# A decayed linear-attention and gated-MLP kernel: split evictions of a PSUM tile, second-product parts in any order, and a new order of all steps

## Chip, cores and metric

The kernel runs on one core of one Trainium2 chip. The metric is the time of one execution in device microseconds. A core has five engines with a queue each, worked through in order: TensorE (PE in the profile, its weight loads PEld), VectorE (DVE), ScalarE (ACT), GpSimd (POOL) and SyncE (SP), which here only issues transfers. POOL issues transfers too; the profile counts both kinds against the same 16 DMA engines.

## The reference, cut to what matters

```python
def _attn_ref(q, k, v, alpha):            # each (4, 8, 768, 48)
    for t in range(S):
        state = alpha[:, :, t, :, None] * state + einsum('bhd,bhe->bhde', k[:, :, t], v[:, :, t])
        y[:, :, t] = einsum('bhd,bhde->bhe', q[:, :, t], state)

def _moe_ref(x, w_in, w_out):             # x (3072, 384), w_in (384, 2048), w_out (2048, 384)
    h = x @ w_in
    g = h * np.cos(h)
    return g @ w_out
```

The output y of the recurrence, heads side by side, is the x of the two products.

## The kernel before

The 3072 rows are worked through as 12 pairs J of 256 rows, three pairs to a batch. A pair consists of two chunks c of 128 rows. Steps of a pair, with the engine that does them:

- `load` (SP): the four inputs a (alpha), k, q, v, 384 KB each. Tiles of a have 4 buffers, those of k, q and v 3 each, so a later load waits until a buffer has been read.
- `w1`, `w2` (POOL): each weight matrix in four loads, cast to bf16 on the way. The number in the plan is the quarter, not the pair.
- `mula` (POOL), `ln` (ACT), `cums0`/`cums` (PE), `sub` (DVE), `icp`, `exps` or together `eb` (ACT): the decay as running sums of logarithms, and its exponentials. `eb` also does the next pair's `ln`.
- `sk`, `sq` (POOL or DVE): k and q scaled by them; `castv` (POOL): v to bf16; `vst` (SP, by transfers inside the core) or `vpe` and `vev` (PE and ACT): v in another layout.
- `trans` (PE) transposes scaled q and k of both chunks into one PSUM tile T_ps of two banks, a bank for each chunk; `evT 0` and `evT 1` copy the banks into qkT, on ACT or DVE.
- `scores` (PE), `mask` (DVE): products of a chunk with itself; `outer` (PE), `add` (DVE), `decay`, `state` (POOL): the state that goes from chunk to chunk.
- `yT` (PE) sums what comes from state and scores into a tile y_ps of two banks; `evy 0` and `evy 1` copy the banks into xT.
- `m1 u` (PE, L361): a quarter u of the first product, 12 matmuls into a PSUM tile h_ps of two banks; `sin` (ACT, L367) takes its cosine as a shifted sine, `gate` (DVE, L372) multiplies the two into gsb.
- `m2 c part` (PE, L390): a quarter of the second product of chunk c, 4 matmuls that add up in o_ps; `evo` copies o_ps to o_sb (ACT or DVE), `out` stores it (SP). The last chunk has two half-width tiles o_last, and is stored in two halves.

The two-bank tiles (T_ps, y_ps, h_ps, U_ps, scores, the early sums) share three PSUM buffers, o_ps has one buffer, and later sums and half of o_last have one. A step that needs a buffer waits for whoever read it last. Two instructions of different engines that use one tile are kept in order by the tile framework.

The order is written out by hand in `PLAN`: each row is a step, each column a pair, and all steps are issued in the order of these numbers (a suffix :A, :D picks ACT or DVE; "-" means that the pair has no such step). A number has no meaning on the chip beyond that order: each engine takes its own steps in turn and waits for data and buffers. `idle` issues matmuls of zeros that keep the TensorE clock up while it has nothing else to do. ACT holds one set of function tables at a time: a `sin` behind an exponential or logarithm, and the other way round, costs a table load (`act_set`).

`GATES` ties the load of a[2] to the last matmul of yT[1]. SP's queue is in order, so every load behind it waits as well:

```python
    GATES, AFTER = {("a", 2): ("yT", 1)}, {}
```

The functions are those of this code:

Of the kernel before, what the change touches and what calls it, by code (L numbers as in the profile page):

```python
# [9 lines left out]
FP = mybir.dt.float32  # L10
# [6 lines left out]
def kernel(  # L17
# [81 lines left out]
    GATES, AFTER = {("a", 2): ("yT", 1)}, {}  # L99
    src = {"a": alpha, "k": k, "q": q, "v": v}  # L100

# [149 lines left out]
    T_ps, A_ps, y_ps, U_ps = {}, {}, {}, {}  # L251

    def trans(J):
        T_ps[J] = ps.tile([C, 2, 2 * NP, 2, HC], BF, tag="h", name="T_ps", bufs=3)
        for i, x in ((1, kh_t[J % NQ]), (0, qh_t[J % NQ])):
            for p in range(NP):
                for e in range(2):
                    for c in range(2):
                        r = slice(HC * c, HC * c + HC)
                        nc.tensor.transpose(T_ps[J][:, c, i * NP + p, e, :],  # L260
                                            x[r, e, 2 * p : 2 * p + 2, :].rearrange("s h d -> s (h d)"), ident_bf[r, r])

    def evict_T(J, c, copy):
        if J not in qkT_sb:
            qkT_sb[J] = sb.tile([C, 2, 2 * NP, C], BF, tag="qkT", name="qkT", bufs=BUF["qkT"])
        copy(out=qkT_sb[J][:, c], in_=T_ps[J][:, c].rearrange("r n e s -> r n (e s)"))  # L266

    def scores(J, c):
        qkT = qkT_sb[J]
        A_ps[J, c] = ps.tile([C, 2, NP, C], FP, tag="h", name="A_ps", bufs=3)  # L270
        for p in range(NP):
            for a in range(2):
                r = slice(64 * a, 64 * a + D)
                nc.tensor.matmul(A_ps[J, c][:, a, p, :], qkT[r, c, NP + p, :], qkT[r, c, p, :], start=True, stop=True)  # L274
# [42 lines left out]
    def yT(J):  # L317
# [25 lines left out]
        for key, step in GATES.items():  # L343
            if step == ("yT", J):
                AFTER[key] = last

    def evict_y(J, c, copy):
        if J not in xT:
            xT[J] = sb.tile([C, KT, T2], BF, tag="xT", name="xT", bufs=BUF["xT"])

        copy(out=xT[J][:, :, c * C : (c + 1) * C].rearrange("r i (t e) -> r i e t", e=2),  # L351
             in_=y_ps[J][:, c, 0 : KT * C].rearrange("r (i e t) -> r i e t", i=KT, e=2))

# [22 lines left out]

    def mlp2(J, c, part):
        if (J, c) == (NJ - 1, 1):
            if part == 0:

                o_ps[J, c] = [ps.tile([C, 512], FP, tag="x", name="o_last", bufs=1), two_banks("o_last")[:, 0]]
            for z, cols in enumerate(HALVES):
                for ft in range(part * NF // MP, (part + 1) * NF // MP):
                    nc.tensor.matmul(o_ps[J, c][z][:, 0 : DM // 2], gsb[J][:, ft, c * C : (c + 1) * C], w2[:, ft, cols],  # L384
                                     start=(ft == 0), stop=(ft == NF - 1))
            return
        if part == 0:
            o_ps[J, c] = ps.tile([C, 512], FP, tag="o", name="o_ps", bufs=1)
        for ft in range(part * NF // MP, (part + 1) * NF // MP):
            nc.tensor.matmul(o_ps[J, c][:, 0:DM], gsb[J][:, ft, c * C : (c + 1) * C], w2[:, ft],  # L390
                             start=(ft == 0), stop=(ft == NF - 1))

    def evict_o(J, c, copy):
# [6 lines left out]
        else:  # L400
            t = sb.tile([C, DM], FP, tag="o_sb", name="o_sb", bufs=4)
            copy(out=t, in_=o_ps.pop((J, c))[:, 0:DM])  # L402
# [9 lines left out]
    def idle(n):  # L412
# [132 lines left out]
```

## Time and profile before

| | us |
|---|---|
| median of 3 runs | 188.44 (188.35 to 189.09) |
| span of the profiled execution | 186.5 |
| TensorE busy in that span | 176.7 |
| ACT and DVE busy | 126.5 and 135.4 |

The span runs from the first to the last instruction of the profiled execution; the runs are timed around it and are some 2 us longer. How time is shared between the two products and the rest, from the page's costliest groups (busy us, mean ns of one, then the idle time of the engine just before them and what ended it):

```profile
L361 PE MATMUL h_ps<-xT,w 128*128 128x256 bf16 x576 | 66.7, 273 | 1.3 <-ACT xT L351 0.7
L390 PE MATMUL o_ps<-w,gsb 128*128 128x384 bf16 x368 | 66.7, 327 | 0.1
L266 ACT COPY qkT<-T_ps 128x1024 bf16<-128x1024 bf16 x8 | 8.0, 1015 | 6.9 <-PE T_ps L260 4.4
L266 DVE COPY qkT<-T_ps 128x1024 bf16<-128x1024 bf16 x16 | 10.8, 678 | 1.1 <-ACT qkT L266 1.1
L351 ACT CAST xT<-y_ps 128x384 bf16<-128x384 f32 x12 | 6.7, 594 | 5.6 <-PE y_ps L340 3.8
L351 DVE CAST xT<-y_ps 128x384 bf16<-128x384 f32 x12 | 6.8, 584 | 4.7 <-PE y_ps L340 2.9
```

A matmul's own time (273 ns) is its way through the array; matmuls overlap, so 12 of them in a row take 1.31 us, and a busy TensorE need not be one at its peak. Where TensorE waits a little, the gap is better read from the starts of its matmuls than from its idle time. The shape of the span, in 40 slices of 4.66 us, each digit a tenth:

```profile
PE   7988799989989999999999999999999999999993
PEclk9999999999999999999999999999999999999999
DMA  6999999999949979996799932600041005301102
```

### The profile page before, as it was taken

How to read it: one execution, taken by the hardware profiler on the slowest of the kernel's cores; microseconds unless marked ns; L12 is line 12 of the kernel's file. 1: busy time of each engine (PE TensorE's matmuls, PEld its weight loads, DVE VectorE, ACT ScalarE, POOL GpSimd, SP SyncE). 2: the span in 40 equal slices, each digit the busy share in tenths (PEclk: the TensorE clock that was granted, in tenths of full speed). 3: DMA queues.
4: the chain of work that ended last, by engine and by line, in shares of the span. 5: the costliest groups of instructions: out<-in, count | busy, mean ns of one | idle time of the engine just before them, and what ended most of it. 6: DMA issues, size and time to landing. Idle time of an engine off the chain costs nothing.

```text
span 186.5 us, 5746 instructions
## 1 busy us (share of the span) xinstructions
PE 176.7 (95%) x2467; PEld 126.4 (68%) x2469; DVE 135.4 (73%) x184; ACT 126.5 (68%) x161; POOL 77.1 (41%) x110
## 2 busy tenths in 40 slices
PE   7988799989989999999999999999999999999993
PEld 2434588655667786785688668676867686786872
DVE  7178775589799979698847987794977556754461
ACT  2466876889498986889668999728965264373330
POOL 5079510257645653781896076930360320100000
PEclk9999999999999999999999999999999999999999
DMA  6999999999949979996799932600041005301102
GB/s 152 261 258 165 181 204 237 259 266 265 274 105 304 264 180 245 264 260 167 186 278 278 247 104 46 182 0 4 4 136 47 5 0 158 118 0 66 64 0 84
DMA packets 60137, 29.47 MB, mean 158 GB/s; under 512 B 51024, under 2 KB 60112, under 8 KB 60112
## 3 DMA queue, kind: packets, MB, share of 16 engines
q1 hardware_dynamic: 56256, 25.86, 57.2%
q0 software_dynamic: 3712, 3.15, 11.0%
q8 instruction: 19, 0.31, 0.7%
q10 hardware_dynamic: 144, 0.10, 0.2%
q14 instruction: 6, 0.05, 0.1%
HBM read 25.17 MB, written 4.72 MB: 160 GB/s over the span
## 4 chain that ended last, share of the span: by engine, by line
PE 73%; ACT 15%; DVE 8%; issue 3%; DVEq 0%
PE h_ps L361 31%; PE o_ps L390 24%; PE idle_ps L416 4%; PE y_ps L340 3%; ACT qkT L266 3%; DVE gsb L372 3%; PE T_ps L260 2%; ACT c_sb L367 2%; PE A_ps L274 2%; ACT L136 2%; ACT cp L200 2%; PE U_ps L291 2%; DVE kh L212 2%; ACT icp L192 2%; PE o_last L384 1%
## 5 line engine op out<-in xcount | busy, mean ns | idle before, releaser
L372 DVE TENSOR_TENSOR gsb<-h_ps,c_sb 128x1024 bf16<-128x1024 f32 x48 | 58.1, 1221 | 21.9 <-ACT c_sb L367 21.2
L367 ACT ACTIVATE c_sb<-h_ps,halfpi 128x1024 bf16<-128x1024 f32 x48 | 53.0, 1113 | 26.8 <-PE h_ps L361 23.0
L361 PE MATMUL h_ps<-xT,w 128*128 128x256 bf16 x576 | 66.7, 273 | 1.3 <-ACT xT L351 0.7
L390 PE MATMUL o_ps<-w,gsb 128*128 128x384 bf16 x368 | 66.7, 327 | 0.1
L361 PEld LDWEIGHTS <-w 128*128 128x128 bf16 x576 | 55.6, 98 | 10.1 <-issue 1.6
L390 PEld LDWEIGHTS <-gsb 128*128 128x128 bf16 x368 | 33.8, 98 | 21.2 <-DVE gsb L372 0.6
L313 POOL TENSOR_TENSOR un<-us,c 128x384 bf16<-128x384 f32 x20 | 16.7, 835 | 40.7 <-DVE us L305 29.1
L279 DVE TENSOR_TENSOR A_sb<-A_ps,msk 128x1024 bf16<-128x1024 f32 x24 | 28.9, 1215 | 1.7 <-PE A_ps L274 1.7
L212 POOL TENSOR_TENSOR kh<-k,icp 128x384 bf16<-128x384 f32 x17 | 16.9, 999 | 9.2 <-ACT icp L192 7.8
L216 POOL TENSOR_TENSOR qh<-q,cp 128x384 bf16<-128x384 f32 x15 | 15.0, 1006 | 11.8 <-ACT cp L200 11.8
L149 POOL TENSOR_TENSOR a<-a 128x384 f32<-128x384 f32 x9 | 9.0, 1001 | 12.6 <-DMA a<-in_alpha_dram 12.6
L219 POOL CAST vp<-v 128x768 bf16<-128x768 f32 x12 | 10.1, 841 | 8.8 <-DMA v<-in_v_dram 7.7
L416 PE MATMUL idle_ps<-zeros 128*128 128x512 bf16 x38 | 12.0, 457 | 1.4 <-DVE zeros L52 1.2
L141 ACT ACTIVATE lna<-a 128x768 bf16<-128x768 f32 x12 | 10.2, 847 | 4.6 <-DMA a<-in_alpha_dram 4.6
L266 ACT COPY qkT<-T_ps 128x1024 bf16<-128x1024 bf16 x8 | 8.0, 1015 | 6.9 <-PE T_ps L260 4.4
L136 ACT ACT_TABLE_LOAD x9 | 11.5, 1283 | 0.9 <-PEq L529 0.7
L367 ACT ACT_TABLE_LOAD x9 | 11.5, 1283 | 0.2
L266 DVE COPY qkT<-T_ps 128x1024 bf16<-128x1024 bf16 x16 | 10.8, 678 | 1.1 <-ACT qkT L266 1.1
L305 DVE TENSOR_TENSOR us<-U_ps,un 128x384 f32<-128x384 f32 x16 | 8.7, 550 | 3.8 <-PE U_ps L291 2.8
L402 DVE COPY o_sb<-o_ps 128x384 f32<-128x384 f32 x12 | 6.6, 551 | 6.5 <-PE o_ps L390 6.5
L351 ACT CAST xT<-y_ps 128x384 bf16<-128x384 f32 x12 | 6.7, 594 | 5.6 <-PE y_ps L340 3.8
L351 DVE CAST xT<-y_ps 128x384 bf16<-128x384 f32 x12 | 6.8, 584 | 4.7 <-PE y_ps L340 2.9
(69 smaller groups left out, 159.1 us busy)
## 6 DMA issues: line engine op xcount, KB each, us to landing
k<-in_k_dram SPq DMA_DIRECT2D x12, 384.0 KB, 6.0
a<-in_alpha_dram SPq DMA_DIRECT2D x12, 384.0 KB, 6.1
v<-in_v_dram SPq DMA_DIRECT2D x12, 384.0 KB, 6.0
q<-in_q_dram SPq DMA_DIRECT2D x12, 384.0 KB, 6.3
out_dram<-o_sb SPq DMA_DIRECT2D x23, 192.0 KB, 2.6
vs<-vp SPq DMA_DIRECT2D x36, 64.0 KB, 2.1
w<-in_moe_w_out_dram POOLq DMA_DIRECT2D x4, 384.0 KB, 10.1
w<-in_moe_w_in_dram POOLq DMA_DIRECT2D x4, 384.0 KB, 7.3
```

The lines of the kernel that those rows point to most:

```text
L136: nc.scalar.preload_act_table_set("natural_log_exp_and_others")
L212: eng.tensor_tensor(out=kh_t[J % NQ][:, e, :, 0:D], in0=kqv["k", J][:, :, e], in1=icp_, op=ALU.mult)
L216: eng.tensor_tensor(out=qh_t[J % NQ][:, e, :, 0:D], in0=kqv["q", J][:, :, e], in1=cp, op=ALU.mult)
L266: copy(out=qkT_sb[J][:, c], in_=T_ps[J][:, c].rearrange("r n e s -> r n (e s)"))
L279: nc.vector.tensor_tensor(out=A_sb[J][:, c].rearrange("s a p t -> s (a p) t"), in0=A_ps.pop((J, c)).rearrange("s a p t -> s (a p) t"), in1 ...
L313: nc.gpsimd.tensor_tensor(out=u, in0=U_sum.pop(n), in1=c2_sb[J][:, :, c].unsqueeze(3).to_broadcast([C, NP, 2, D]), op=ALU.mult)
L351: copy(out=xT[J][:, :, c * C : (c + 1) * C].rearrange("r i (t e) -> r i e t", e=2), in_=y_ps[J][:, c, 0 : KT * C].rearrange("r (i e t) -> ...
L361: nc.tensor.matmul(h_ps[J, u][:, f, :], w1[:, kk, ft * C : (ft + 1) * C], xT[J][:, kk, :], start=(kk == 0), stop=(kk == KT - 1))
L367: nc.scalar.activation(out=c_sb[J, u], in_=h_ps[J, u], func=AF.Sin, bias=halfpi, scale=1.0)
L372: nc.vector.tensor_tensor(out=gsb[J][:, u * FW : (u + 1) * FW], in0=h_ps.pop((J, u)), in1=c_sb.pop((J, u)), op=ALU.mult)
L390: nc.tensor.matmul(o_ps[J, c][:, 0:DM], gsb[J][:, ft, c * C : (c + 1) * C], w2[:, ft], start=(ft == 0), stop=(ft == NF - 1))
L416: nc.tensor.matmul(idle_ps[0], zeros[:, 0:C], zeros, start=True, stop=True)
```

## The change

Four things, in the diff below.

1. `apart` tells the tile framework that the copies of a tile's two banks do not depend on each other where two engines do them (evict_T and evict_y).
2. `mlp2` counts the parts of a chunk that have been issued: the first to come starts the sum and takes the tile, the fourth ends it. Before, part 0 had to be first and part 3 last. (The tile of o_ps is now kept in a list; `evict_o` takes the first.)
3. `GATES` is empty: no load waits for a step of TensorE. Its use is moved to `pass_gate`, which may also be tied to a scores step; with no gate it does nothing.
4. Every row of `PLAN` has new numbers, and the engine of some evictions and scalings is another. `evT` is on ACT 10 times (8 before), `evy` 9 times (12 before), `evo` 13 times (11 before); `sk` and `sq` are on POOL 36 times (32 before). The two evictions of a pair are on two engines in 13 of 24 cases. There are 33 idle matmuls (38 before), and 14 changes of ACT's tables (18 before).

```diff
-    GATES, AFTER = {("a", 2): ("yT", 1)}, {}
+    GATES, AFTER = {}, {}
+    def pass_gate(step, last):
+        for key, gate in GATES.items():
+            if gate == step:
+                AFTER[key] = last
...
+    evicts = {}
+    def apart(key, copy, ins):
+        if key in evicts and evicts[key][0] != copy:
+            tc.declare_no_dep(ins.ins, evicts[key][1].ins, reason="two engines each evict a bank of their own")
+        evicts[key] = copy, ins
...
     def evict_T(J, c, copy):
-        copy(out=qkT_sb[J][:, c], in_=T_ps[J][:, c].rearrange("r n e s -> r n (e s)"))
+        ins = copy(out=qkT_sb[J][:, c], in_=T_ps[J][:, c].rearrange("r n e s -> r n (e s)"))
+        apart(("T", J), copy, ins)
...
     def evict_y(J, c, copy):
-        copy(out=xT[J][:, :, c * C : (c + 1) * C].rearrange("r i (t e) -> r i e t", e=2),
+        ins = copy(out=xT[J][:, :, c * C : (c + 1) * C].rearrange("r i (t e) -> r i e t", e=2),
              in_=y_ps[J][:, c, 0 : KT * C].rearrange("r (i e t) -> r i e t", i=KT, e=2))
+        apart(("y", J), copy, ins)
...
     def mlp2(J, c, part):
+        last_tile = (J, c) == (NJ - 1, 1)
+        done = parts_done[J, c] = parts_done.get((J, c), 0) + 1
+        if done == 1:
+            if last_tile:
                 o_ps[J, c] = [ps.tile([C, 512], FP, tag="x", name="o_last", bufs=1), two_banks("o_last")[:, 0]]
+            else:
+                o_ps[J, c] = [ps.tile([C, 512], FP, tag="o", name="o_ps", bufs=1)]
+        fts = range(part * NF // MP, (part + 1) * NF // MP)
+        for o, cols in zip(o_ps[J, c], HALVES if last_tile else [slice(0, DM)]):
+            for ft in fts:
+                nc.tensor.matmul(o[:, 0 : cols.stop - cols.start], gsb[J][:, ft, c * C : (c + 1) * C], w2[:, ft, cols],
+                                 start=(done == 1 and ft == fts[0]), stop=(done == MP and ft == fts[-1]))
...
 PLAN = {
-    "load a": "1320 1974 27415 27985 34270 40270 43270 54870 67336 68770 70970 93397",
-    "load k": "750 2544 28555 37270 46270 52480 58570 69470 72470 85140 91627 113474",
-    "load q": "5250 6750 29125 38770 48970 56370 57870 60070 78470 84570 87104 96187",
-    "load v": "3750 8250 35770 41770 51910 61570 67906 73970 75470 85710 95267 96757",
-    "w1": "15334 12769 17804 16954",
-    "w2": "11919 20284 19434 21134",
-    "evT 0": "14773:A 18473:A 41585 48048 60976 71899 81566:A 93894 111044 116949:A 129834 138061",
-    "evT 1": "16453:A 19403:A 43330 48048:A 59896 72979 81586 93289 112124 117657 128759 137201:A",
-    "yT": "20503 26545 48000 58219 72693 91349 90719 109104 124433 140168 151138 162701",
-    "evy 0": "21333:D 27535:D 49128:D 60501:D 73683 92814:D 91919 110094:D 125423 140998 152879:D 163777:D",
-    "evy 1": "21333 27658 48990 59421:D 73683:D 92339:D 91549 110569:D 125793 141368 152128 163814",
-    "m1 0": "23356 30719 52864 63871 77482 95445 98081 113200 130658 146436 158652 170128",
-    "m1 1": "22038 32037 51246 65489 74546 94127 92809 121714 129340 147754 154722 171446",
-    "m1 2": "27430 29401 54182 61235 78800 96763 104369 120396 132629 149072 159970 166198",
-    "m1 3": "25132 33355 55500 62553 76164 99399 110564 111882 136796 145118 161288 172764",
-    "m2 0 0": "28748 41460 56818 70639 84360 100717 114518 125318 138114 150390 163586 174082",
-    "m2 0 1": "34673 42113 57471 71292 85013 101670 115171 125971 138767 152023 164239 176046",
-    "m2 0 2": "35326 42766 59519 71945 85666 103063 116824 128034 139420 153416 164892 176699",
-    "m2 0 3": "35979 44554 60172 73893 86619 103716 117477 128687 140893 154069 165545 177352",
-    "evo 0": "36832:D 45407 61581:D 78353:D 87472 105178:D 118330 129540 141746 154922:D 166398:D 178205:D",
-    "out 0": "47770 53670 76970 97327 92197 114044 134921 150722 154222 155552 167028 178835",
-    "out 1": "44770 66136 87674 100827 112274 133721 136121 156752 149522 168228 170958 180161",
...
+    "load a": "30 10 560 580 900 1370 1560 2530 2620 3110 3750 2320",
+    "load k": "180 340 620 940 1570 2140 2680 2440 3280 4470 4150 4200",
+    "load q": "250 390 780 1050 1390 2370 2120 2930 3580 2270 3480 4870",
+    "load v": "70 530 890 1360 1530 3210 3020 3140 3850 4400 4660 4420",
+    "w1": "440 300 660 520 - - - - - - - -",
+    "w2": "1100 930 980 760 - - - - - - - -",
+    "evT 0": "290:A 490:A 1460:A 1720 2260 2800 3100:A 3620 4330 4620:A 5060:A 5520",
+    "evT 1": "360 480:A 1400 1700:A 2250 2750 3170 3600:A 4350 4640 5090 5530:A",
+    "yT": "510 740 1730 2110 2770 3640 3630 4300 5020 5210 5670 5950",
+    "evy 0": "590:D 810:D 1790:D 2130:D 2790 3690 3660:D 4320:D 5040 5240 5680 5980:D",
+    "evy 1": "540 750:D 1740:D 2210:D 2820:D 3700 3670:D 4310:D 5030:D 5250:D 5730 6020",
+    "m1 0": "790 860 1960 2490 2980 3790 3920 4550 5170 5620 5870 6380",
+    "m1 1": "720 1060 1800 2510 2850 3710 3680 4920 5370 5840 6160 6080",
+    "m1 2": "850 1030 2000 2230 3030 3860 4170 4910 5390 5920 5890 6270",
+    "m1 3": "840 970 2040 2410 2950 3940 4490 4440 5180 5600 6050 6260",
+    "m2 0 0": "1110 1420 2070 2710 3310 3990 4690 5340 5700 6100 6330 6520",
+    "m2 0 1": "1090 1540 2050 2840 3320 3960 4530 5080 5590 6120 6310 6500",
+    "m2 0 2": "1070 1500 2180 2740 3330 4020 4710 5350 5820 6130 6340 6490",
+    "m2 0 3": "990 1380 2280 2730 3270 4130 4720 5120 5720 6070 6350 6550",
+    "evo 0": "1130:D 1550 2300:D 2910:D 3410 4160 4730:D 5360 5830:D 6140:D 6360 6570",
+    "out 0": "3260 2390 2760 4480 3720 4830 6320 5970 6410 6290 6370 6580",
+    "out 1": "3390 2290 3070 4970 4000 5000 5460 5490 6150 6250 6510 6610",
...
 }
-IDLE = [(1501, 16), (7915, 1), (9416, 8), (12569, 4), (14554, 5), (16389, 3), (18254, 3)]
+IDLE = [(45, 14), (215, 9), (415, 6), (465, 1), (505, 1), (695, 2)]
```

In the new order SP's queue begins a1, a0, v0, k0, q0, k1, q1, v1, a2, a3, k2, q2, v2, a4, k3, q3, v3, a5 (before: k0, a0, a1, k1, v0, q0, q1, v1, then the gate, a2, a3, k2, q2, a4). The weights come as w1 quarters 1, 0, 3, 2 and w2 quarters 3, 1, 2, 0 (before: w2[0], then w1 1, 0, 3, 2, then w2 2, 1, 3). TensorE's first units and parts after yT[0] are m1.1[0], yT[1], m1.0[0], m1.3[0], m1.2[0], m1.0[1], m1.3[1], m2.0.3[0], m1.2[1], m1.1[1], m2.0.2[0], m2.0.1[0], m2.0.0[0], cums0[2].

More of the change, by code (lines that the diff above doesn't have):

```diff
@@ L273, in scores @@
                 r = slice(64 * a, 64 * a + D)
-                nc.tensor.matmul(A_ps[J, c][:, a, p, :], qkT[r, c, NP + p, :], qkT[r, c, p, :], start=True, stop=True)
+                last = nc.tensor.matmul(A_ps[J, c][:, a, p, :], qkT[r, c, NP + p, :], qkT[r, c, p, :], start=True, stop=True)
+        pass_gate(("scores", J, c), last)
     def mask(J, c):
@@ L342, in yT @@
             begun.add((c, g))
-        for key, step in GATES.items():
-            if step == ("yT", J):
-                AFTER[key] = last
+        pass_gate(("yT", J), last)
     def evict_y(J, c, copy):
@@ L375 @@
     HALVES = [slice(0, DM // 2), slice(DM // 2, DM)]
+    parts_done = {}
     def mlp2(J, c, part):
-        if (J, c) == (NJ - 1, 1):
-            if part == 0:
+        last_tile = (J, c) == (NJ - 1, 1)
+        done = parts_done[J, c] = parts_done.get((J, c), 0) + 1
+        if done == 1:
+            if last_tile:
                 o_ps[J, c] = [ps.tile([C, 512], FP, tag="x", name="o_last", bufs=1), two_banks("o_last")[:, 0]]
[L382 to L391, printed above, removed]
+            else:
[5 more added lines that the diff above has]
+                                 start=(done == 1 and ft == fts[0]), stop=(done == MP and ft == fts[-1]))
     def evict_o(J, c, copy):
@@ L401, in evict_o @@
             t = sb.tile([C, DM], FP, tag="o_sb", name="o_sb", bufs=4)
[L402 removed]
+            copy(out=t, in_=o_ps.pop((J, c))[0][:, 0:DM])
             o_sb[J, c] = [(t, slice(0, DM), nc.sync)]
```

2 lines of the change are left out of this document (1 added, 1 removed), and 84 rows, old and new, of the table PLAN.

## The prediction, made before the changed kernel ran

> **What bounds the kernel now.** I read the page's busy table first, then the busy time by stage, then the chain of waits, then what the transfers did in the first 40 us.
>
> ```profile
> PE 176.7 (95%) x2467; PEld 126.4 (68%) x2469; DVE 135.4 (73%) x184; ACT 126.5 (68%) x161; POOL 77.1 (41%) x110
> ...
> 0.00:22.20 22.20, 18.24 (x242) 9.18 (x245) 14.46 (x41) 12.03 (x19) 13.15 (x31) 1.00 1.08 205
> 22.20:36.85 14.65, 14.36 (x168) 11.72 (x168) 9.17 (x10) 11.77 (x11) 1.82 (x2) 1.00 1.25 229
> 36.85:53.34 16.49, 15.06 (x252) 9.55 (x252) 14.76 (x20) 13.01 (x22) 8.56 (x12) 1.00 1.05 250
> 53.34:120.00 66.66, 65.68 (x974) 49.04 (x973) 54.88 (x70) 56.90 (x71) 42.51 (x52) 1.00 0.89 213
> 120.00:186.50 66.50, 63.33 (x833) 46.92 (x832) 42.09 (x47) 32.78 (x40) 11.05 (x15) 1.00 0.15 48
> ```
>
> The columns after the stretch are PE, PEld, DVE, ACT, POOL, clock, DMA share and GB/s. TensorE sets the end. The clock is full throughout, and from 53 us on TensorE idles about 1 us before the last matmul. The change removes no real matmul (only 38 to 33 idle ones, all before 22 us), so all it can move is when the first h_ps matmul starts (22.20), what the transfers hold up before 53 us, and the small stalls behind. DMA share 1.25 and 1.05 says that the 16 engines are saturated between 22 and 53 us: whatever is loaded earlier makes something else later.
>
> The waits of one evicting engine for the other, and two of the stalls that end at TensorE:
>
> ```profile
> ACT qkT L266 <- DVE qkT L266: 2.4, 1, 2.4
> ACT xT L351 <- DVE xT L351: 1.8, 3, 0.8
> DVE xT L351 <- ACT xT L351: 1.8, 2, 1.1
> DVE qkT L266 <- ACT qkT L266: 1.1, 2, 0.9
> PE h_ps L361 <- ACT xT L351: 0.7, 1, 0.7
> PE U_ps L291 <- DVE xT L351: 0.6, 1, 0.6
> ```
>
> **Eviction pairs.** These rows add up to 7.1 us of one engine waiting for the other, but only 0.7 + 0.6 us arrive at TensorE by name: at 22.20 (DVE evicts xT from 20.94 for 0.59, ACT only from 21.56 for 0.59, then h_ps) and at 52.07. In the new order 13 of the 24 qkT and xT pairs are split over two engines. No row shows two engines reading one tile's two banks at once. Bounds: a pair ends with the slower copy (1015 ns on ACT beside 678 on DVE; 594 beside 584 for xT), or, if they hinder each other fully, as late as now, a gain of nothing. I take the first; each copy has a bank of its own.
>
> **The start.** Each input load takes 1.5 us (393 KB at 261 GB/s, the rate between 9 and 13 us). By place in the queue they land in before at 4.42, 5.94, 7.45, 8.95, 10.44, 11.95, 13.46. In the new order a1, a0, v0, k0, q0, k1, q1, v1: k0 waits until 8.95 instead of 4.42, q0 comes at 10.44 instead of 11.95. Walk with the durations of before: ln[0] ends 6.80 as now; icp.0, exps.0 of pair 0 and exps.0 of pair 1 run before the second-bank sums, and the sums wait for them (tile dependence, in the built program's waits), so exps.1[0] ends about 9.6 and icp.1[0] 11.1. DVE then does sk.1, sq.1, sq.0 of pair 0 (0.55 each) to 12.75; trans[0] ends 13.2 (now 14.32), scores.0[0] waits for ACT's evT.0 (1.02) and vev (0.8), both at 15.05 (now 16.11); the masks (1.21 each) end 18.2; yT[0] ends 19.0 (now 20.91). mask.0[1], which frees the bank, ends at 20.8, so the first h_ps matmul is possible at 20.85: 1.35 us earlier. This is the gain that the idle matmuls, the split evictions and the load order give together.
>
> **The gate that goes.** GATES held the load of a[2], and with it every later load on SP's queue, until yT[1]. Without it SP issues a2, a3, k2, q2, v2, a4 ... without a pause, and the eight weight loads on POOL's queue meet them. Before had them apart:
>
> ```profile
> 27.24 0.99 SPq L105 DMA_DIRECT2D a<-in_alpha_dram  x2
> ...
> 18.89 2.29 POOL L127 DMA_DIRECT2D w<-in_moe_w_out_dram  x3
> ...
> q0 software_dynamic: 624, 0.47, 131.4%
> ...
> q1 hardware_dynamic: 614, 0.23, 107.9%
> q0 software_dynamic: 9, 0.01, 5.5%
> ```
>
> The first two lines are the issues (SP's input loads, POOL's last weight loads); the third is the queue table between 28.4 and 30.7 us, weights alone; the last two between 31.6 and 32.4. A weight load is 512 packets of 768 B, so alone it takes 512 / (624 / 2.3) = 1.89 us; one engine sends a packet each 59 ns (2300 x 16 / 624). In the last window one engine still has weights, and beside the input packets it sends 9 in 800 ns, one each 89 ns: the queues alternate there packet by packet. Then a weight load takes 512 / 16 x 89 = 2.85, say 2.9 us with inputs beside it, and meanwhile the inputs get 512 packets of 384 B, half a load.
>
> The Trainium skill ("DMA: Bandwidth & Descriptors", Queues, rings and completion order) says each DMA engine goes round robin between queues at packet granularity. The last window agrees (89 ns); the earlier window does not: loads issued at 27.24 had no packet by 30.7. By the rule alone the weights would take the 2.9 us worked out above.
>
> POOL's new order is castv[0] (from 7.5), decay, sk.0[0] (to 10.9), then w1[1]; its packets start about 2 us after the issue (12.45 to 14.1 in before). The next two weights stand behind state.0[0], decay[1], sk.1[1], sq.0[1] (add.0[0] ends 13.25; then 0.85 + 0.25 + 1.0 + 1.0 give 16.4), the fourth behind castv[1] and state.1[0], the others behind the next states. So w1[1] comes at 16.5, in time; the other seven flow from about 19 us, 7 x 2.9 = 20.3, to 39.3, with 0.4 to land: w1[0] 22.3, w1[3] 25.2, w1[2] 28.1, w2[3] 31.0, w2[1] 33.9, w2[2] 36.8, w2[0] 39.7. In before the last lands at 32.8 (issued at 20.42, 12.4 us). TensorE does m1.1[0], yT[1], m1.0[0] to 24.7, waits for w1[3] and w1[2], runs five units and one part to 35.25, waits for w2[2] and for w2[0]; m2.0.0[0] (0.65) ends at 40.35, and only then cums0[2] follows, in before at 36.85. **Term 1: +3.5 us**, with the 1.35 of the start swallowed by it. Queued behind the waiting matmuls is all of TensorE; ACT and DVE starve with it.
>
> **36.85 to 53.34.** Here before pays for the gate: gaps between matmul starts are 3.0 us (0.8 before trans[2]'s q half, 0.75 before U_ps at 52.07, the rest 0.1 to 0.3 each). In the new one a2, a3, k2, q2, v2 have landed by then; the total of bytes is the same, so k3 and q3 come where they came (42.7 and 44.2; k3 at 42.99 in before, q3 about 1.5 later). Walked from 40.35 in the new order, TensorE waits for sq.0[2] behind exps.0[2] (0.3), for sq.0[3] behind mask.1[2] on DVE (0.5) and for evT.0[3] (0.2): 1.0 instead of 3.0. **Term 2: -2.0.**
>
> **The rest.** From 53 us the gaps between starts come to 2.1 us in before (0.43 at 76.5 for the second xT eviction, 0.52 at 86.4 and 0.46 at 119.6 for a late gate behind qkT evictions and table loads, the rest under 0.3). The split pairs and 14 instead of 18 switches between exponent and sine tables (4 x 1283 ns of ACT, hidden in the last stretch, where ACT is busy 32.78 of 66.5) take those away: -2.1. New ones: the order is dense and much is moved at once, q[9] is loaded before q[5] and a[11] before a[7], holding one of three and one of four buffers, and q[5] stands on SP behind out.1[1], which waits for an eviction near 57 us. Bounds for new stalls: 0.5 (the stretch from 120 to the last matmul has that) to 4 (the rate of 36.85 to 53.34 for a third of the way). I take 1.7, near the stretch it resembles. **Term 3: -0.4.** The tail is the same: two o_last halves last, both orders.
>
> **Sum.** 186.5 + 3.5 - 2.0 - 0.4 = 187.6 us of span; the median of the runs, 188.44, lies 1.9 above the span: 189.5 us. Own range 187.5 to 192.
>
> **Rivals.** (1) *The weights are not held up.* For it: the window without any input packet while weights flowed. Against: the 89 ns. Then seven loads from 18.2 at 1.95 end at 32.3, TensorE works through from 23.4 (eight units at 1.31, parts at 0.65, one short wait) to 35.2 instead of 40.35; the inputs of pair 3 are needed 5 us earlier and still come just in time. 189.5 - 5.15 = 184.4 us, faster than before. It decides as soon as w1[2] lands before 25 us.
> (2) *Transfers go in order of issue.* The same window speaks for it. w1[0], issued at 16.4, then waits for everything SP issued before it, through q2 or v2, and the later weights for the loads issued between: last weight near 42.7, +3.0: 192.5 us. If a queue went on until it is empty, it would be worse still: 22 loads at 1.5 us.
> (3) *The pairs stay in line* (the declared independence does nothing): the 0.6 and the stalls of term 3 come back: +1.6, 191.1 us. The built program has no wait between the two copies, so this is unlikely.
>
> **How the numbers follow.** A measurement of this kernel can tell about 0.5% from no change, here 187.5 to 189.4. Forecast 0.57, rival 1 0.22, rival 2 0.17, rival 3 0.04. Faster: nearly all of rival 1 and a fifth of the forecast's spread, 0.32. Same: 0.28 of the forecast and a little of the others, 0.17. Slower: 0.51. The range 184.0 to 194.0 takes in half of rival 1, the bounds of term 3 and most of rival 2.
>
> **What would show it.** Right: first h_ps matmul near 21; between 20 and 39 us both queues in every window, weights near two thirds of 203 GB/s; TensorE waiting for weights at m1.3[0], m1.2[0] and in the second product of pair 0; cums0[2] near 40; ACT and DVE copies of one tile side by side; stalls of 1 us, not 3, up to 54 us. Wrong: cums0[2] before 37 (rival 1) or after 42 (rival 2), or more than 4 us of new gaps behind 54 us.

## The result, and the profile after

The changed kernel takes 189.65 us (189.43 to 189.96, five runs); the kernel before, beside it on the same chip, 188.46 us (188.35 to 189.09, five runs). The ratio is 1.0061 (95% interval 1.0043 to 1.0078): slower by 0.6%, or 1.2 us. The profiled execution of the changed kernel spans 187.9 us, that of before 186.5.

The page's busy line, and two of the groups of evictions:

```profile
PE 174.4 (93%) x2462; PEld 125.5 (67%) x2462; DVE 133.3 (71%) x180; ACT 122.4 (65%) x157; POOL 82.4 (44%) x114
...
L278 ACT COPY qkT<-T_ps 128x1024 bf16<-128x1024 bf16 x10 | 10.0, 1012 | 7.4 <-PE T_ps L272 7.2
L278 DVE COPY qkT<-T_ps 128x1024 bf16<-128x1024 bf16 x14 | 9.3, 680 | 0.2 <-PE T_ps L272 0.2
```

In these copies both engines now wait for the transposes alone, and no longer for each other (before: DVE 1.1 us behind ACT, ACT 2.4 us behind DVE); a copy takes what it took (1012 and 680 ns against 1015 and 678). The busy time by stage, cut at the same points of the work in both kernels: the first h_ps matmul, the start of cums0[2] (the first running sums of pair 2), the start of cums[5], the end. Changed kernel, columns as in the prediction:

```profile
0.00:20.94 20.94, 17.39 (x237) 8.62 (x238) 12.35 (x39) 11.68 (x18) 12.66 (x30) 1.00 1.12 232
20.94:41.70 20.76, 14.83 (x172) 11.50 (x169) 10.08 (x11) 11.83 (x11) 5.67 (x7) 1.00 1.23 216
41.70:58.26 16.56, 15.71 (x265) 10.24 (x262) 15.31 (x20) 11.94 (x21) 11.06 (x13) 1.00 0.75 172
58.26:187.88 129.62, 126.47 (x1799) 95.18 (x1795) 95.55 (x111) 86.94 (x109) 53.06 (x65) 1.00 0.52 133
```

and the last two stretches of the kernel before, cut at the same two points:

```profile
36.85:54.48 17.63, 16.20 (x262) 10.57 (x262) 15.90 (x21) 14.13 (x23) 9.32 (x13) 1.00 1.00 238
54.48:186.54 132.06, 127.87 (x1797) 94.95 (x1794) 95.83 (x114) 88.56 (x110) 52.80 (x66) 1.00 0.52 132
```

Up to cums0[2] the change loses 41.70 - 36.85 = 4.85 us. From there to cums[5] it gains 17.63 - 16.56 = 1.07, and over the rest 132.06 - 129.62 = 2.44. Together +1.34, the difference of the spans. The second stretch has as many matmuls as before (some 170 in 20.76 us instead of 14.65), and TensorE idles in 5.9 us of it. The waits at TensorE name what it waited for (us in total, times, longest):

```profile
PE h_ps L374 <- DMA w<-in_moe_w_in_dram: 3.1, 3, 1.2
PE o_ps L403 <- DMA w<-in_moe_w_out_dram: 2.9, 2, 1.6
...
PE T_ps L272 <- DVE qh L221: 0.9, 1, 0.9
```

TensorE's timeline from 24 us shows each of the five waits (start, duration, in brackets the idle time before it):

```profile
24.07 1.49 PE L374 MATMUL h_ps<-xT,w 128*128 128x256 bf16 x12 [0.75 <-DMA w<-in_moe_w_in_dram]
26.68 1.48 PE L374 MATMUL h_ps<-xT,w 128*128 128x256 bf16 x12 [1.12 <-DMA w<-in_moe_w_in_dram]
29.37 4.10 PE L374 MATMUL h_ps<-xT,w 128*128 128x256 bf16 x36 [1.21 <-DMA w<-in_moe_w_in_dram]
...
38.04 1.46 PE L403 MATMUL o_ps<-w,gsb 128*128 128x384 bf16 x8 [1.30 <-DMA w<-in_moe_w_out_dram]
41.06 0.81 PE L403 MATMUL o_ps<-w,gsb 128*128 128x384 bf16 x4 [1.55 <-DMA w<-in_moe_w_out_dram]
```

The eight weight loads land at 19.1, 24.0, 26.6, 29.3, 32.2, 35.2, 38.0 and 41.0 us; in before they had landed at 17.7 to 32.8. What the engines carried meanwhile, from the queue table between 24 and 38 us (q0 is POOL's queue with the weights, q1 SP's with the inputs; packets, MB, share of 16 engines):

```profile
q0 software_dynamic: 2419, 1.92, 85.9%
q1 hardware_dynamic: 2422, 0.92, 37.4%
```

One packet of inputs for each packet of weights, over 14 us. And the pair of xT evictions at 18.7 us, which ran one behind the other in before, in the timeline of the changed kernel:

```profile
18.68 0.59 DVE L363 CAST xT<-y_ps 128x384 bf16<-128x384 f32 x1 [0.74 <-PE y_ps L354]
...
18.84 0.60 ACT L363 CAST xT<-y_ps 128x384 bf16<-128x384 f32 x1
```

### The profile page after: what moved, and what is told of

Read it like the earlier page. It is cut to its first block, busy times and chain, and to the rows that moved or that the text cites. A ratio compares the mean times of both kernels' runs of the same rounds, so it can differ in the third digit from the quotient of the medians.

```text
span 187.9 us, 5727 instructions
## 1 busy us (share of the span) xinstructions
PE 174.4 (93%) x2462; PEld 125.5 (67%) x2462; DVE 133.3 (71%) x180; ACT 122.4 (65%) x157; POOL 82.4 (44%) x114
## 4 chain that ended last, share of the span: by engine, by line
PE 81%; DMA 8%; POOL 4%; DVE 2%; ACT 1%; issue 1%; DVEq 0%; POOLq 0%
PE o_ps L403 31%; PE h_ps L374 28%; DMA w<-in_moe_w_out_dram 8%; PE y_ps L354 4%; PE idle_ps L429 4%; PE A_ps L287 3%; PE T_ps L272 3%; PE U_ps L305 2%; PE o_last L403 1%; POOL un L327 1%; POOL w L132 1%; DVE A_sb L293 1%; ACT qkT L278 1%; PE cums_h L160 1%; PE cums L160 1%
## 5 line engine op out<-in xcount | busy, mean ns | idle before, releaser
L380 ACT ACTIVATE c_sb<-h_ps,halfpi 128x1024 bf16<-128x1024 f32 x48 | 53.2, 1113 | 29.3 <-PE h_ps L374 29.1
L374 PE MATMUL h_ps<-xT,w 128*128 128x256 bf16 x576 | 67.7, 273 | 3.1 <-DMA w<-in_moe_w_in_dram 3.1
L403 PE MATMUL o_ps<-w,gsb 128*128 128x384 bf16 x368 | 67.7, 327 | 2.9 <-DMA w<-in_moe_w_out_dram 2.9
L403 PEld LDWEIGHTS <-gsb 128*128 128x128 bf16 x400 | 36.7, 98 | 23.6 <-issue 3.3
L327 POOL TENSOR_TENSOR un<-us,c 128x384 bf16<-128x384 f32 x20 | 16.9, 853 | 36.5 <-DVE us L319 24.1
L221 POOL TENSOR_TENSOR qh<-q,cp 128x384 bf16<-128x384 f32 x19 | 19.6, 1046 | 16.8 <-ACT cp L205 16.8
L278 ACT COPY qkT<-T_ps 128x1024 bf16<-128x1024 bf16 x10 | 10.0, 1012 | 7.4 <-PE T_ps L272 7.2
L363 DVE CAST xT<-y_ps 128x384 bf16<-128x384 f32 x15 | 8.2, 585 | 7.1 <-PE y_ps L354 7.1
L415 ACT COPY o_sb<-o_ps 128x384 f32<-128x384 f32 x12 | 5.7, 478 | 10.4 <-PE o_ps L403 9.6
L217 DVE TENSOR_TENSOR kh<-k,icp 128x384 bf16<-128x384 f32 x7 | 5.5, 785 | 6.5 <-ACT icp L197 6.5
L287 PE MATMUL A_ps<-qkT 48*128 48x128 bf16 x192 | 9.0, 218 | 0.8 <-ACT vs L244 0.4
L278 DVE COPY qkT<-T_ps 128x1024 bf16<-128x1024 bf16 x14 | 9.3, 680 | 0.2 <-PE T_ps L272 0.2
```

What stands on the lines that cost most here:

```text
L217: eng.tensor_tensor(out=kh_t[J % NQ][:, e, :, 0:D], in0=kqv["k", J][:, :, e], in1=icp_, op=ALU.mult)
L221: eng.tensor_tensor(out=qh_t[J % NQ][:, e, :, 0:D], in0=kqv["q", J][:, :, e], in1=cp, op=ALU.mult)
L278: ins = copy(out=qkT_sb[J][:, c], in_=T_ps[J][:, c].rearrange("r n e s -> r n (e s)"))
L287: last = nc.tensor.matmul(A_ps[J, c][:, a, p, :], qkT[r, c, NP + p, :], qkT[r, c, p, :], start=True, stop=True)
L327: nc.gpsimd.tensor_tensor(out=u, in0=U_sum.pop(n), in1=c2_sb[J][:, :, c].unsqueeze(3).to_broadcast([C, NP, 2, D]), op=ALU.mult)
L374: nc.tensor.matmul(h_ps[J, u][:, f, :], w1[:, kk, ft * C : (ft + 1) * C], xT[J][:, kk, :], start=(kk == 0), stop=(kk == KT - 1))
```

## The experiments

Theory: the loss is the gate that went, by the alternation of the two queues, and the rest of the change is a gain. Rivals: the new order itself is slow (POOL's order, the parts), or the two copies of a pair still run in line (one behind the other), or the weights would be late with the gate too. Each kernel was timed beside the kernel before; its ratio has a 95% interval in brackets. The runs stand in three groups on three chips, in which before took 188.53, 188.30 and 188.41 us; across groups the ratios compare better than the times.

| kernel | us | ratio to before |
|---|---|---|
| changed, gate on a[2] put back | 186.4 | 0.9898 [0.9868, 0.9929] |
| changed, gate on k[2] | 186.4 | 0.9899 [0.9875, 0.9922] |
| changed, pairs in line again | 195.45 | 1.0380 [1.0354, 1.0406] |
| before, without its gate | 192.93 | 1.0254 [1.0220, 1.0287] |
| before, pairs side by side | 186.21 | 0.9901 [0.9878, 0.9923] |
| changed, gate on a[2], weights issued early | 184.62 | 0.9821 [0.9789, 0.9852] |
| changed, no gate, weights issued early | 188.04 | 0.9988 [0.9978, 0.9997] |
| changed, gate on a[3], weights issued early | 184.22 | 0.9772 [0.9751, 0.9793] |
| the same, six result buffers | 184.19 | 0.9776 [0.9755, 0.9796] |
| changed, parts ascending, first time | 190.70 | 1.0135 [1.0082, 1.0188] |
| the same, second time | 191.58 | 1.0164 [1.0142, 1.0186] |
| changed, beside these | 189.81 | 1.0067 [1.0048, 1.0086] |

### The gate put back, on a[2] or on k[2]

```
-    GATES, AFTER = {}, {}
+    GATES, AFTER = {("a", 2): ("yT", 1)}, {}
-        "load a": "30 10 560 580 900 ...
+        "load a": "30 10 741 742 900 ...
-        "load k": "180 340 620 940 ...
+        "load k": "180 340 743 940 ...
-        "ln": "40 20 690 1220 ...
+        "ln": "40 20 1085 1220 ...
```

The second kernel leaves a[2], a[3] and ln[2] where the changed kernel has them, and gates k[2] (at 743), and with it all that SP issues later.

> The changed kernel with the old gate back (the load of a[2], and all behind it on SP, waits for yT[1]; ln[2] goes behind sin.1[1] on ACT, so that ACT does not wait for a[2]). Theory: what the change loses is that inputs and weights share the DMA engines. Then the seven weight loads behind w1[1] land 1.9 to 2 us apart instead of 2.9, the last near 33 instead of 41, and cums0[2] starts at 36 +-0.7 instead of 41.7. The inputs of pairs 2 and 3 come late again, so 1 to 2 us go back before 58 us: 186.5 us in all (185.5 to 188). Rival (the weights are late for another reason, POOL's order say, or what the gate gives is all paid back by pairs 2 and 3): cums0[2] may move, the time does not, 189 or more.

> The changed kernel with a gate one load pair later: a[2] and a[3] go ahead of the weights, k[2] and all behind it waits for yT[1]. Theory: only 3 us of inputs stand before the weights, and these meet the first one alone; cums0[2] at 36.5 +-0.8, pair 2 ready earlier than with the gate on a[2]: 185.7 us (184.5 to 187.3). Rival (any input ahead of the weights costs its full 1.5 us at the end of the weights): 1 to 2 us slower than with the gate on a[2].

Measured: 186.4 us both. The gate is worth 3.2 us in the new order (3.1 by the ratios), and the two places of it are the same, so the rival of the second expectation falls. Since the second kernel leaves ln[2] in its place, the move of ln[2] in the first isn't what gains. The stages of the kernel with a[2] gated:

```profile
20.74:38.32 17.58, 14.60 (x173) 11.50 (x170) 10.08 (x11) 11.94 (x11) 4.66 (x6) 1.00 1.21 204
38.32:54.79 16.47, 15.72 (x263) 10.23 (x262) 14.69 (x20) 11.93 (x21) 11.42 (x14) 1.00 1.17 261
54.79:184.43 129.64, 126.51 (x1799) 95.26 (x1795) 95.57 (x111) 86.94 (x109) 53.17 (x65) 1.00 0.53 136
```

The last two stretches are those of the changed kernel within 0.1 us (16.56 and 129.62); all of the 3.4 us of span comes ahead of cums0[2]. But the expectations were too good there: cums0[2] came at 38.32, not at 36 (with k[2] gated at 38.55, not at 36.5), and the last weight at 37.6, not at 33. The gate opens at 23.2 us in this order; POOL issues its last four weights only at 21.8 to 24.9 us. From 27 us on the inputs flow beside them, and the last three land 2.9 to 3.0 us apart.

### The gate taken out of before

```
-    GATES, AFTER = {("a", 2): ("yT", 1)}, {}
+    GATES, AFTER = {}, {}
```

> The kernel before, with the gate taken out and nothing else. Theory: its weights then share the engines with a2, a3, k2, q2, v2 as the changed kernel's do; its last weight lands near 39 to 41 instead of 32.8, cums0[2] starts 2.5 to 4.5 us late, pairs 2 and 3 give 1 to 2 us of it back: 190.5 us (189.5 to 192). Rival (the gate is no matter, the new order alone costs the time): 188.5 +-0.4.

Measured: 192.93 us, 4.4 above the runs of before beside it (188.53) and above the range of the theory: nothing is given back. (Two of its four runs, 193.05 and 193.47 us, have a mean clock of 0.991; the other two take 192.76 and 192.81. The last section comes back to this.) The rival falls. Weights land at 21.1 to 40.45 us (before 17.7 to 32.8), cums0[2] at 41.1 (36.85), and the list of waits has a line that before has not:

```profile
PE h_ps L361 <- DMA w<-in_moe_w_in_dram: 4.7, 4, 2.1
```

### The pairs: in line in the new order, side by side in the old one

```
-        if key in evicts and evicts[key][0] != copy:
+        if False and evicts[key][0] != copy:
```

> The changed kernel without the declared independence: two engines evict the banks of a tile one after the other again. Theory: the 13 pairs are 0.6 to 1 us later each; up to 42 us the late weights hide it, behind that some reach TensorE: 191 us (190.2 to 192). Rival (the pairs are off the path everywhere): 189.6 +-0.4.

Measured: 195.45 us, 5.8 above the changed kernel; expected 1.4. cums0[2] is at 41.63 as in the changed kernel, so none of it is at the start; the stages behind grow from 16.56 to 17.70 and from 129.62 to 134.27. The waits of one evicting engine for the other are 17.7 us in this kernel (7.1 in before, none in the changed kernel):

```profile
DVE qkT L278 <- ACT qkT L278: 5.6, 5, 1.5
...
DVE xT L363 <- ACT xT L363: 4.7, 3, 2.0
ACT xT L363 <- DVE xT L363: 4.4, 2, 3.0
...
ACT qkT L278 <- DVE qkT L278: 3.0, 2, 2.2
```

The opposite edit gives the kernel before the same declaration, and nothing else:

```
+        ins = copy(out=qkT_sb[J][:, c], in_=T_ps[J][:, c].rearrange("r n e s -> r n (e s)"))
+        apart(("T", J), copy, ins)
...
+        apart(("y", J), copy, ins)
```

> The kernel before, with one thing of the change alone: its qkT and xT eviction pairs are declared independent where two engines share them; gate, order and parts stay. Theory (the pairs cost by the stalls that they end at TensorE in the trace of before, 0.6 at 22.2, 0.75 at 51.3, 0.4 at 76.5, 0.5 at 86.4): about 2 us off, 186.3 us (185.5 to 187.3), first h_ps matmul near 21.6. Rival A (the old order was laid out around the wait, and what is gained is lost a little later): 188.0 to 188.7. Rival B (worth as much as in the new order, 5.8 us): 183 us.

Measured: 186.21 us, the first h_ps matmul at 21.66: the theory, and both rivals fall. Its gain is 2.1 us of time (188.30 beside it) and 2.3 of span: 0.5 at the start, and 0.95 and 0.92 in the two late stages, which are:

```profile
36.45:53.13 16.68, 15.94 (x263) 10.52 (x263) 15.61 (x22) 14.14 (x23) 10.41 (x14) 1.00 1.06 258
53.13:184.27 131.14, 127.48 (x1797) 94.77 (x1794) 95.47 (x113) 88.59 (x110) 52.41 (x65) 1.00 0.52 133
```

So side by side is worth 2.1 us in the old order and 5.8 in the new one. And the old order with it takes 186.2 us with its gate (0.9901 of before), the new one with a gate 186.4 (0.9898): with both of these equal, **the new order by itself brought nothing** that these runs can tell. From the stages: it gains 0.9 until the first h_ps matmul (20.74 against 21.66), 0.2 and 1.5 in the late ones (16.47 and 129.64 against 16.68 and 131.14), and loses 2.8 between the first h_ps matmul and cums0[2] (17.58 against 14.79).

### The weights issued as soon as POOL can

That loss of 2.8 should be POOL's order: POOL issues weights at 10.7 and then from 16.3 to 24.9 us, in before from 12.4 to 20.4. The next two kernels issue them as early as POOL is free, with the gate on a[2] and without any:

```
-        "w1": "440 300 660 520 ...
-        "w2": "1100 930 980 760 ...
+        "w1": "305 300 525 520 ...
+        "w2": "764 664 762 662 ...
```

> The changed kernel with the gate of a[2] put back and the eight weight loads issued as early as POOL's own work lets them, in the order in which TensorE uses them. Theory (what the weights cost is the inputs beside them; once these are held and POOL issues in time, a load takes 1.9 to 2.0 us): last weight lands at 31 to 33, cums0[2] at 35 to 36.5, PE waits for no weight after the second one, 183.5 us (182.5 to 185). Rival (the weights' own queue on POOL needs its 2.5 us each whatever is issued when, as in the run with the gate alone): as with the gate alone, 186.4 us, last weight near 37.

> The changed kernel without any gate, with the same early issue of the weights. Theory (inputs on SP's queue still alternate with the weights packet by packet): the loads still come about 2.9 us apart while inputs flow, but from an earlier start, so the last lands at 37 to 39, cums0[2] at 38.5 to 40, 187.5 us (186 to 189). Rival (only the late issue on POOL hurt, not the sharing): as fast as the run with gate and early issue, 183.5 us.

Measured: 184.62 and 188.04 us. Early issue is worth 1.8 us with the gate and 1.6 without, the gate 3.2 and 3.4 (by the ratios 1.5 and 1.4, 3.1 and 3.1): the two add up, and neither stands for the other; both rivals fall. Of the loss of 2.8 us up to cums0[2], early issue takes back 1.9: with the gate that stage is 15.68 us now (20.88 to 36.56), for 17.58 without early issue and 14.79 in the old order. Without the gate the last weight lands at 39.7 and cums0[2] follows at 40.4, both just behind the expected range. With it the time is as expected but the way there is not: the last weight lands at 34.8, not at 31 to 33. In the timeline of TensorE around cums0[2],

```profile
34.82 0.81 PE L403 MATMUL o_ps<-w,gsb 128*128 128x384 bf16 x4 [0.32 <-DMA w<-in_moe_w_out_dram]
36.56 0.32 PE L160 MATMUL cums_h<-lna,tri 128*128 128x384 bf16 x1 [0.93 <-ACT lna L146]
```

the weights cost 0.3, and then a[2], landed at 34.4 beside the last weights, holds up ln[2].

### The gate one load later, and more result buffers

Against the kernel with the gate on a[2] and early weights:

```
-    GATES, AFTER = {("a", 2): ("yT", 1)}, {}
+    GATES, AFTER = {("a", 3): ("yT", 1)}, {}
-        "load a": "30 10 741 742 900 ...
+        "load a": "30 10 560 742 900 ...
-        "ln": "40 20 1085 1220 ...
+        "ln": "40 20 690 1220 ...
```

and for the other kernel also

```
-            t = sb.tile([C, DM], FP, tag="o_sb", name="o_sb", bufs=4)
+            t = sb.tile([C, DM], FP, tag="o_sb", name="o_sb", bufs=6)
```

> As the run with gate and early weights, but a[2] is loaded freely right behind the first eight inputs (as in the changed kernel), and the gate sits one load later, on a[3]; ln[2] stands where the changed kernel has it. Theory (the DMA engines are the limit of the first 50 us; the stall of 1.1 us at cums0[2] is a[2] landing late, at 34.4, and 0.9 us in which the engines were nearly idle around 18 us are to be had): a[2] lands near 17.3, the last weight at 34 to 35.5, cums0[2] at 35.5 to 36.2, 183.8 us (183.2 to 184.5). Rival (a[2] costs the weights what it gains for itself): the wait moves to the parts of the second product, cums0[2] at 36.5 or later, 184.6 us or more.

> The same with six buffers for the result tiles instead of four. Theory (the wait of 0.8 us at 64 us, where VectorE evicts a result, is for the store of an earlier result, which lands at 64.4 behind the inputs on SP's queue, and not for TensorE as the list of waits has it): that wait and the two small ones behind it go, 1.0 to 1.6 us less than with four buffers, 182.6 us (182 to 183.3). Rival (the wait is for something else, or comes back as the next late input): as with four buffers, within 0.4 us.

Measured: 184.22 us, 0.9772 [0.9751, 0.9793] of before: below both kernels, by 4.2 and by 5.6 us (188.41 and 189.81 beside it). That it beats the gate on a[2] isn't clear, since the two intervals meet (0.9789 there, 0.9793 here). With six result buffers it is the same. The time is in the theory's range, its steps are not: a[2] lands at 20.8 (expected 17.3), the last weight at 35.6, cums0[2] at 36.28. The wait for ln[2] is gone; a wait for the last weight has taken its place, 1.4 us: that much of the rival is right, but its 184.6 us isn't. The stages:

```profile
20.67:36.28 15.61, 14.26 (x173) 11.58 (x169) 10.14 (x11) 12.31 (x11) 4.39 (x6) 1.00 1.25 221
36.28:52.83 16.55, 15.70 (x264) 10.23 (x262) 15.31 (x20) 11.93 (x21) 11.04 (x13) 1.00 1.06 243
52.83:182.46 129.63, 126.50 (x1799) 95.22 (x1795) 95.58 (x111) 86.95 (x109) 53.15 (x65) 1.00 0.53 135
```

Against the changed kernel only the first of these differs, 15.61 for 20.76: 5.15 of the 5.4 us of span (the rest lies ahead of it, 20.67 for 20.94). While the gate holds the inputs, between 20 and 26 us, the queue table of this kernel reads

```profile
q0 software_dynamic: 1389, 1.21, 125.6%
...
q1 hardware_dynamic: 5, 0.00, 0.2%
```

weights alone, 0.20 MB a us instead of the 0.14 of the changed kernel; its last three weights, beside the inputs again, land 2.8 to 3.0 us apart. Six result buffers changed nothing (184.19): that expectation falls, and the run can't tell whether the wait at 64 us was for a store, since the kernel with four buffers no longer has that wait. It stood in the one profiled execution of the kernel with a[2] gated and early weights, the slowest of that kernel's four (185.7).

### The parts of the second product in ascending order

```
-        "m2 0 0": "1110 1420 2070 2710 ...
-        "m2 0 3": "990 1380 2280 2730 ...
+        "m2 0 0": "990 1380 2070 2710 ...
+        "m2 0 3": "1110 1540 2280 2840 ...
...
-        "w2": "1100 930 980 760 ...
+        "w2": "760 930 980 1100 ...
```

> The changed kernel with the four parts of the second product in ascending order in 23 of the 24 tiles (the one left has a gate in between), and the four quarters of w2 loaded in that order too; no matmul more or less. Theory (the order of the parts is bookkeeping: each part is the same eight matmuls, and TensorE meets its gate a little earlier or later): 189.6 us, within 0.7. Rival (the free order hides late gates: each gate that is still under way when its part comes is a stall): 190.7 us or more, with new waits of o_ps for gsb in the list of waits.

> The kernel with ascending parts once more, beside the changed kernel on one chip, since its first four times spread by 2.2 us while its profile had the same marks as that of the changed kernel within 0.1 us. Theory (order of parts is worth nothing): within 0.4 us of the changed kernel. Rival (it costs what the first four times said): 0.7 us or more above the changed kernel.

> The changed kernel itself, to be read beside the three others of this call: 189.65 us within 0.4, and the kernel with ascending parts within 0.4 of it (theory) or 0.7 above it (rival).

Measured: 190.70 us (189.75 to 191.91) and 191.58 us (191.24 to 191.70), beside 189.81 for the changed kernel. The first profile, of a run of 189.75 us, has every mark of the changed kernel within 0.1 us, and no wait of o_ps for gsb: order costs nothing there. The second profile, of a run of 191.70 us, is the same up to 38.97 us; then comes an idle stretch of TensorE of 2.15 us, and the clock falls. Its timeline, and its windows (clock third from the right):

```profile
38.16 0.81 PE L403 MATMUL o_ps<-w,gsb 128*128 128x384 bf16 x4 [0.69 <-DMA w<-in_moe_w_out_dram]
41.11 1.44 PE L403 MATMUL o_ps<-w,gsb 128*128 128x384 bf16 x4 [2.15 <-DMA w<-in_moe_w_out_dram]
42.35 0.53 PE L160 MATMUL cums_h<-lna,tri 128*128 128x384 bf16 x1
```

```profile
37.05:40.45 3.40, 1.23 (x7) 0.51 (x6) 0.00 (x0) 2.20 (x2) 0.00 (x0) 1.00 1.21 251
40.45:43.85 3.40, 2.74 (x15) 1.36 (x15) 1.26 (x2) 0.00 (x0) 0.00 (x0) 0.50 1.14 252
43.85:47.25 3.40, 3.37 (x44) 2.13 (x41) 2.86 (x4) 2.85 (x6) 2.24 (x4) 1.00 1.05 258
```

The same window of the first profile, at full clock:

```profile
40.45:43.85 3.40, 2.88 (x25) 1.84 (x25) 2.04 (x3) 1.21 (x4) 0.25 (x1) 1.00 1.19 258
```

15 matmuls at clock 0.50 for 25 at 1.00: cums[5] starts at 60.3 instead of 58.3, and nothing of it comes back. So the theory is right where the clock stays and wrong in the median, and the rival has the size but the wrong cause: no gate is waited for. In the changed kernel the same lateness of w2 is two waits of 1.30 and 1.55 us, with eight matmuls between them; ascending, it is 0.69 and 2.15. Of the ascending kernel's eight runs six have a mean clock of 0.991 and take 191.2 to 191.9 us, two have 1.00 and take 189.75 and 189.99; of the changed kernel's eleven none is below 0.997.

Why the first profile, with the same idle stretch of 2.15 us, keeps its clock, the clock record of the traces shows. In all fourteen traces the clock changes only whole multiples of 3.413 us after its first rise: in the second profile it rises at 6.31, falls ten such windows later at 40.44, and is back one window after that. On this grid the window ahead of the fall has TensorE busy for 1.25 us, 0.37 of it. In the first profile the rise is at 5.24, so a border of the grid cuts the idle stretch, and the emptier of the two windows that share it still has 1.81 us, 0.53 (first line below); in the changed kernel the emptiest one ahead of the tail has 1.46 us, 0.43 (second line):

```profile
39.37:42.78 3.41, 1.81 (x18) 1.17 (x18) 0.97 (x2) 0.14 (x1) 0.00 (x0) 1.00 1.21 283
37.62:41.03 3.41, 1.46 (x8) 0.78 (x8) 0.00 (x0) 1.56 (x2) 0.00 (x0) 1.00 1.21 263
```

Of the windows that lie whole in the fourteen traces, the clock fell behind each of the four in which TensorE was busy for 0.37 or less (the three others are in the tails), and behind none with 0.43 or more. Slid along the trace from 8 us to the tail, such a window is never emptier than 0.43 in the changed kernel; with ascending parts, some six tenths of the possible starts of the grid would put a window below 0.40. So the split of the wait decides whether the clock can fall, and the start of the grid whether it does; that last is an estimate from the busy times, since the split wasn't varied further.

## Why the prediction came out right

The time, 189.65 for 189.5, is this close by luck, because three mis-sized terms cancelled: 187.6 of span, + 1.35 (term 1) + 0.93 (term 2) - 2.04 (term 3) = 187.84; measured 187.88. The sign is owed to term 1, and its mechanism is shown.

- **The start (-1.35, swallowed).** First h_ps matmul at 20.94, predicted 20.85. It was swallowed by the weights, as said.
- **Term 1 (+3.5): +4.85.** The mechanism holds: the gate put back gives 3.2 us; taken out of before, it costs 4.4. Spacing of the weights from w1[0] on: 2.6, 2.7, 2.9, 3.0, 2.8, 3.0 us, predicted 2.9. (It took 512 packets of 768 B for every load; the trace has 384 packets of 1 KB for a quarter of w1, which come closer: at some 150 packets a us beside the inputs these take 2.6 us, 512 packets at some 180 a us take 2.9.) What was off is the start of the chain, "its packets start about 2 us after the issue": w1[0], issued at 16.47, had almost no packets until 20.2 us, so it landed at 24.0 instead of 22.3, and all behind it 1.2 to 1.4 us late. In that gap a[3] and k[2] went ahead of it, as rival 2 had it. The same step was off for w1[1]: issued at 10.87, it had its first packet at 14.45 and shared the engines with a[2], and landed at 19.1 instead of 16.5; it was needed only at 20.94. The prediction also put the whole term down to the gate; POOL's later issue of the weights is part of it, 1.6 us by the run without a gate and with early weights.
- **Term 2 (-2.0): -1.07.** The stalls went where expected; the wait for sq.0[3] is there, but 1.0 us long instead of 0.5 (it stands as 0.9 of qh in the waits), so it alone fills the 1.0 that all the new stalls were to take, and the small distances between starts stayed. Of the 1.07, the pairs alone bring 0.95 in the old order (16.68 us in before with pairs side by side).
- **Term 3 (-0.4): -2.44** (here from cums[5] on, some 1 us behind the prediction's border). The old stalls went (2.1 estimated), and no new ones came: the 1.7 taken for the dense order was wrong. Behind 58 us one distance between starts is more than 0.1 us too long (0.14, at 110 us). Of the 2.44, the pairs bring 0.9 in the old order (stage 131.14 for 132.06 in before with pairs side by side), and the new order another 1.5. That split holds only in this sequence: taken out of the new order, the pairs cost 4.65 us of this stage (134.27 for 129.62), more than the whole gain.
- **Rival 1 (weights not held up, 184.4)** would have shown weights alone between 20 and 32 us; both queues flow in equal packets. Its sum matches another kernel, 184.2 with the inputs held and the weights early, but its steps don't: there the last weight lands at 35.6, not at 32.3.
- **Rival 2 (order of issue, 192.5)** holds for 3 to 4 us after a new arrival, as far as these traces go, and not after that; the last weight landed at 41.0, between the 39.7 of the forecast and its 42.7.
- **Rival 3 (pairs in line, 191.1).** The pairs do run side by side. Its price was far too low, 1.6 for a measured 5.8: it was the 0.6 at the start and the stalls of term 3, all read from before, and the new order leans on the pairs more than the old one.

The change in sum, by the ratios and in this sequence: pairs side by side 0.9901 of before (-1.9 us), then order and parts 0.9898 (nothing clear of noise), then the gate gone 1.0061 (+3.1).

## What to carry to other kernels

When a change lifts a gate on loads, ask first which other loads will then flow beside them, count packets and not bytes, and look at when the loads that are needed first are issued: here the gate was worth 3.1 to 3.4 us, and issuing the weights early another 1.4 to 1.8. What a part of a change is worth depends on the order it stands in (the pairs 5.8 us in the new order, 2.1 in the old one), so its price is read from the kernel in which it will run, by taking it out there. If something must be late, two short waits with work between them can cost less than one long one where the clock can fall (here 189.8 us for 191.6).

## What the runs showed of the hardware

**Two queues share the engines in equal numbers of packets, but not at once.** Packets in each us of the changed kernel, counted from the trace, by the time at which they start:

| us | 14 | 15 | 16 | 17 | 18 | 19 | 20 | 21 | 22 | 23 | 24 |
|---|---|---|---|---|---|---|---|---|---|---|---|
| weights (q0) | 33 | 143 | 142 | 78 | 4 | 1 | 140 | 200 | 192 | 139 | 152 |
| inputs (q1) | 587 | 155 | 144 | 484 | 834 | 711 | 241 | 29 | 46 | 140 | 152 |

w1[1], issued at 10.87, has its first packets at 14.45, beside a[2]. w1[0] was issued at 16.47 and waits until a[3] and k[2], issued before it, have passed at 20.2; then the weights pass almost alone for two us, though q[2], whose issue runs from 15.15 to 19.15, and v[2], issued at 19.19, are waiting; from 23 us on the two go one for one again. In before the inputs issued at 27.24 had their first packets at 30.8, when the weights were all but through. The Trainium skill ("DMA: Bandwidth & Descriptors", Queues, rings and completion order) says that each engine goes round robin over its queues at packet granularity: the equal counts between 24 and 38 us (2419 and 2422 packets) fit that, though they don't show how many packets pass between two switches; the 3 to 4 us after a queue's new loads don't fit. What makes that delay isn't settled.

**The granted clock can halve behind an idle stretch of 2.15 us.** It fell 1.5 us into it, at 40.45, and came back 3.4 us later (windows above). In the 3.4 us before the fall TensorE was busy for 1.23 us. The Trainium skill ("TensorE: Matmul & The Clock Gate", Part 1: The HAM clock gate) puts the fall after an idle window of about 3.4 us, on a free-running window: the length of the slow stretch agrees, and so does the grid of 3.413 us, but a window that is 0.37 busy was enough here, and one of 0.43 was not. The same idle stretch in another execution, cut by a border of the grid, left the clock at 1.00. The kernel before without its gate, with a wait of 2.14 us ahead of its first h_ps matmul, has a mean clock of 0.991 in two of four runs, as one half-clock window in 191 us gives. A lower mean clock didn't always cost time: 0.988 stands beside 185.95 us, the fastest of the four runs with the gate put back on a[2], and 0.991 beside 188.08 and 187.84 us without a gate and with early weights (188.04 in the median); none of these three was profiled, so where their clock was down isn't known.

**Two engines read two banks of a PSUM tile at full speed**: 0.59 and 0.60 us side by side for xT at 18.7 us; for qkT, the two copies that both start at 131.70 us take 1012 ns on ACT and 691 on DVE, beside means of 1012 and 680.

**Open:** in the kernel with a[2] gated the weights came 2.4 to 2.6 us apart while alone on the engines (between 19 and 24 us 815 packets, 0.80 MB), and in before 1.8 to 2.65 us (928 packets, 0.91 MB in the same window), so that the prediction's 1.89 us for a load alone is near the fast end. Why isn't known. A gate that opens later than yT[1], which would spare the last three weights of the best kernel, wasn't tried.
